# Reordering the ramp of batch 0 in a retention-plus-mixer kernel

## The chip, the cores and the metric

The kernel runs on one core of a Trainium2 chip. The metric is the time on the device, in microseconds, from the start to the end of the program; smaller is better. The numbers come from two sources: three timed runs, and one execution that the hardware profiler recorded. The engines are called PE (TensorE: matmuls and transposes), DVE (VectorE), ACT (ScalarE), POOL (GpSimd) and SP (SyncE, which here only issues transfers).

## What is computed

The inputs are q, k and v of shape 4 x 8 x 768 x 64 (batch, head, time, feature) in fp32, and four weights. A retention layer runs over time, and its output goes through a low-rank token mixer and a two-layer MLP with a residual:

```python
gamma = 1.0 - 2.0 ** (-5.0 - np.arange(H))
for t in range(S):
    state = gamma[None, :, None, None] * state + np.einsum('bhd,bhe->bhde', k[:, :, t], v[:, :, t])
    y[:, :, t] = scale * np.einsum('bhd,bhde->bhe', q[:, :, t], state)
...
h = xt @ U @ V                       # xt: x with time and features exchanged; rank 32 over 768 steps
u = x + h.transpose(0, 2, 1)
return u + np.maximum(u @ w_ch1, 0.0) @ w_ch2      # 512 -> 2048 -> 512
```

## The kernel before

**Chunks.** Each batch's 768 time steps are six chunks of 128. The recurrence is done chunk by chunk with matmuls. For chunk c, `ret_k` (L262) scales k by a decay (`kd`), `ret_q` or `ret_q0` scales q (`qd`), `ret_v` (L274) casts v on ACT (`vb`). kd and qd are transposed by PE (`kT`, `qT`), `ret_S` (L347) multiplies them into scores, `ret_mask` (L361) masks the scores on DVE in two halves of 0.68 us (`a`), `ret_sum` (L392) adds k times v of this chunk to one running PSUM bank, `ret_state` (L403) turns that bank into the masked bf16 `state` on DVE, and `ret_O` (L367) makes the chunk's output from qT with the state of the chunk before and from `a` with vb; ACT evicts it (`x`, L385). Since all six chunks add to one bank, `ret_sum` of chunk c+1 waits until `ret_state` of chunk c has read it.

**The ramp.** Before the first MLP matmul, batch 0 needs all its chunks, the low-rank product (`mix_P`, which needs `Ub`, and `mix_x`, `mix_h`, which need `Vb`) and the first columns of w1. This stretch is written out by hand at L564 to L641: the order of the calls is the order of the instructions on each engine, and each engine works strictly in that order. In batch 0 the loads of q come in pairs of chunks, 512 KB each, with even and odd rows apart (`load_q0`, L173); `ret_q0(i, eng)` (L302) scales the even half on one engine and the odd half on the other, `ret_Tq0(i, eng)` (L310) transposes both into one bank and evicts them into `q0T` with one strided copy of 1024 columns, by DVE for pair 0 and by ACT for pairs 1 and 2. `ret_Tk0(c)` (L324) transposes kd and evicts kT with ACT. `run_idle(n)` (L194) issues n matmuls on zeros into a bank that nobody reads. `cast_v` (L248) casts the mixer's V to bf16 on DVE; `spread_v` (L251) spreads it with PE and ACT.

**Queues.** All loads of batch 0 are issued by SP in the order of the list at L178: k0, q pair 0, k1, k2, V, q pair 1, k3, v0, q pair 2, k4, v1, k5, v2 to v5, then U. w1 and w2 are loaded and cast by POOL's own queue (`load_w1`, `load_w2`). At L601 POOL first copies one column of a v tile into `Ub`, so that the w1 loads behind it are not issued until that tile has landed; then come two w1 loads, `setup_u` (which waits for U), and the rest. POOL carries out in order: kd of each chunk, one half of each q pair, that gate, the weight loads, and later kd and qd of the other batches.

**The other batches.** The MLP of batch b runs as 32 slots of four matmuls (`mlp1`) and 48 slots of mostly two (`mlp2`); the retention of batch b+1 is put between them by slot number (`S_at`, `O_at`, `mix_at`, L644 to L680). The loads of batch 1 wait for a one-column ACT instruction at slot 14 of batch 0 (L138). From batch 2 on the transposes are done by DMA, issued by SP (L296); the scores of chunks 2 and 3 are put at slot 36.

Of the kernel before, what the change touches and what calls it, by code (L numbers as in the profile page):

```python
# [10 lines left out]
bf16 = mybir.dt.bfloat16  # L11
AF = mybir.ActivationFunctionType
# [35 lines left out]
def kernel(  # L48
# [20 lines left out]
    NP = H // 2  # L69
# [84 lines left out]
    Ub = wts.tile([P, NCK, RK], bf16)  # L154
# [16 lines left out]
    t0 = {}  # L171
# [3 lines left out]
        nc.sync.dma_start(out=q0f[:, i].rearrange("p h e d -> p h (e d)"),  # L175
                          in_=q[0, :, ds(2 * P * i, 2 * P)].rearrange("h (p e) d -> p h (e d)", e=2))

    for what in ("k0", "q0", "k1", "k2", "V", "q1", "k3", "v0", "q2", "k4", "v1", "k5", "v2", "v3",  # L178
                 "v4", "v5"):
        if what == "V":  # L180
            nc.sync.dma_start(out=Vf, in_=moe_V)
        elif what[0] == "q":
            load_q0(int(what[1]))
        else:
            load_one(t0, 0, int(what[1]), k if what[0] == "k" else v, what[0] + "_n")
# [8 lines left out]
    def run_idle(n):  # L194
        w = bank(0)
        for _ in range(n):
            matmul(w, idle[:, :P], idle, DM, start=True, stop=True)
# [50 lines left out]
    def cast_v():  # L248
        nc.vector.tensor_copy(out=Vs, in_=Vf)
# [24 lines left out]
    def ret_v(b, c):  # L274
        vb = rmid.tile([P, H, D], bf16, tag="vb", name=f"vb_{b}_{c}", bufs=6)
        nc.scalar.activation(vb, rc[b, c]["v_n"], AF.Copy)  # L276
        bal.book("A", 0.63)
        rc[b, c]["vb"] = vb
# [23 lines left out]
    def ret_q0(i, eng):  # L302
        t0["qd", i] = []
        for e in (0, 1):
            d = rmid.tile([P, H, D], bf16, tag="qd", name=f"qd0_{i}_{e}", bufs=4)
            eng[e].tensor_tensor(d, t0["q", i][:, :, e],  # L306
                                 Gq0[:, 2 * i + e].unsqueeze(2).to_broadcast([P, H, D]), op=ALU.mult)
            t0["qd", i].append(d)

    def ret_Tq0(i, eng):  # L310

        tp = bank(1, bf16, 2 * DM)
        for e, d in enumerate(t0["qd", i]):
            for n in range(NP):
                nc.tensor.transpose(tp[:, ds(e * DM + n * P, P)], d[:, ds(2 * n, 2)], ident)
                bal.mm(P)
        o = q0T[:, :, ds(2 * P * i, 2 * P)].rearrange("p n (t e) -> p e n t", e=2)
        src = tp.rearrange("p (e n t) -> p e n t", e=2, n=NP)
        if eng == "A":
            nc.scalar.activation(o, src, AF.Copy)  # L320
        else:
            nc.vector.tensor_copy(out=o, in_=src)

    def ret_Tk0(c):  # L324
        r = rc[0, c]
        o = rmid.tile([P, NP, P], bf16, tag="qkT", name=f"kT_0_{c}", bufs=6)
        tp = bank((2, TP)[c % 2], bf16, 2 * DM)[:, :DM]
        for p in range(NP):
            nc.tensor.transpose(tp[:, ts(p, P)], r["kd"][:, ds(2 * p, 2)], ident)
            bal.mm(P)  # L330
        r["kT"], r["qT"] = o, q0T[:, :, ts(c, P)]
        nc.scalar.activation(o.rearrange("p n t -> p (n t)"), tp, AF.Copy)  # L332

    def ret_T(b, c):
        if by_dma(b):
# [11 lines left out]
    def ret_S(b, cs, masks=True, bks=(SA, SB)):  # L347

        for c, bks in zip(cs, (bks, (OB, TP if by_dma(b) else 2))):
            r = rc[b, c]  # L350
            r["s"] = [bank(i) for i in bks]
            for p in range(NP):
                for e in (0, 1):
                    matmul(r["s"][e][:, ts(p, P)], r["kT"][ds(D * e, D), p],
                           r["qT"][ds(D * e, D), p], 80, start=True, stop=True)
        for c in cs:
            rc[b, c]["a"] = rmid.tile([P, 2, NP, P], bf16, tag="a", name=f"a_{b}_{c}", bufs=5)
            for e in (0, 1) if masks else ():
                ret_mask(b, c, e)

    def ret_mask(b, c, e):  # L361
        r = rc[b, c]
        nc.vector.tensor_tensor(r["a"][:, e], r["s"][e].rearrange("p (n t) -> p n t", n=NP), mask4,  # L363
                                op=ALU.mult)
        bal.book("V", 0.69)
# [197 lines left out]

    ret_k(0, 0, G)  # L564
    ret_Tk0(0)
    run_idle(3)
    ret_q0(0, (V, G))
    ret_Tq0(0, "V")
    ret_k(0, 1, G)
    ret_Tk0(1)  # L570
    run_idle(3)
    ret_S(0, [0])
    ret_k(0, 2, G)
    ret_Tk0(2)
    ret_S(0, [1], bks=(OB, ST))
    run_idle(4)
    ret_q0(1, (G, V))
    ret_Tq0(1, "A")
    ret_k(0, 3, G)
    ret_Tk0(3)  # L580
    cast_v()
    run_idle(2)
    ret_S(0, [2])
    ret_v(0, 0)
    spread_v()
    ret_sum(0, 0)
    ret_state(0, 0)
    ret_q0(2, (G, V))
    ret_S(0, [3])
    run_idle(2)  # L590
    ret_Tq0(2, "A")
    ret_k(0, 4, G)
    ret_v(0, 1)
    ret_Tk0(4)
    ret_O(0, 0, False)
    run_idle(2)
    ret_sum(0, 1)
    ret_state(0, 1)
    ret_k(0, 5, G)

    nc.gpsimd.tensor_copy(out=Ub[:, 0, :1], in_=t0["v_n", 2][:, 0, :1])  # L601
    load_w1(0, 256)
    load_w1(256, 256)
    setup_u()
    load_w1(512, 512)
    ret_S(0, [4])
    ret_Tk0(5)
    run_idle(1)
    ret_v(0, 2)
    ret_O(0, 1, False)  # L610
    ret_sum(0, 2)
    ret_state(0, 2)


    c = NCK - 3
    ret_v(0, c)
    ret_S(0, [NCK - 1], masks=False)
    ret_mask(0, NCK - 1, 0)
    ret_v(0, c + 1)
    ret_sum(0, c)  # L620
    ret_state(0, c)
    ret_O(0, c - 1, False)
    ret_mask(0, NCK - 1, 1)
    ret_O(0, c, False, (TP,))
    ret_v(0, c + 2)
    ret_sum(0, c + 1)
    ret_state(0, c + 1)
    ret_O(0, c + 1, False)
    for cc, bk in ((0, 1), (1, 2), (2, SA), (3, TP)):
        mix_x(0, 0, cc, bk)  # L630
    ret_O(0, c + 2, False, (SB, 0))
    mix_P(0, list(range(NCK - 1)), (OB, ST))
    mix_P(0, [NCK - 1])
    for cc, bk in ((0, SB), (1, 0)):
# [9 lines left out]
    for b in range(B):  # L644
        nxt = b + 1 < B
        slots = mlp1_slots(b)
        n1 = len(slots)
        side = {}
        set_banks([0, 1, 2, SA, SB, OB])
        if b == 0:  # L650
            taken.update({i: n for n, i in enumerate((1, 2, SA, TP, SB, 0, OB))})
            set_banks([1, 2, SA, TP, SB, 0, OB])
            order = [0, 2, 1, 3] + list(range(4, len(slots)))
            slots = [slots[i] for i in order]
            for i, s in ((1, 2), (2, 3)):
                put(side, i, lambda s=s: load_w1(512 * s, 512))
            for s in range(4):
                put(side, 4 + s, lambda s=s: load_w2(s))
            for c in range(NCK):
                put(side, 14, lambda c=c: load_chunk(1, c))  # L660
            at, lead, mix_at = [n1 + 7 + 5 * c for c in range(NCK)], 4, n1 + 38
            S_at = {(0, 1): n1 + 14, (2, 3): n1 + 24, (4,): n1 + 30, (5,): n1 + 35}
            O_at = [n1 + i for i in (19, 22, 29, 32, 35, 38)]
        if b:

            slots = slots[:12:2] + slots[1:12:2] + slots[12:]
        if b and nxt:
            set_banks([0, 1, 2])
            at, lead, mix_at = [10 + 4 * c for c in range(NCK)], 5, n1 + 24
            S_at = {(0, 1): 27, (2, 3): 36, (4, 5): 46}  # L670
            O_at = [32, 35, 42, 45, 52, 55]
        if nxt:
            ret_side(b + 1, at, lead, S_at, O_at, side)
            put(side, n1, lambda: set_banks([0, 1], [2]))
            put(side, mix_at, lambda: use.update(mix=[2, SA, SB]))
            mix_side(b + 1, mix_at, side)
        if b == 1:
            for c, i in ((3, 0), (4, 7), (5, 15)):
                put(side, i, lambda c=c: load_chunk(2, c))
        weave(slots + mlp2_slots(b), side)  # L680
# [30 lines left out]
```

## Time and profile before

| what | us |
|---|---|
| three timed runs, median (lowest to highest) | 231.39 (230.69 to 231.39) |
| profiled execution: its own time | 231.24 |
| profiled execution: span from first to last instruction | 229.5 |
| first matmul of the MLP of batch 0 starts at | 31.18 |
| PE busy in the span | 219.4 (96%) |
| ACT, DVE, POOL busy in the span | 113.8, 82.3, 55.2 |

The 1.7 us between the time and the span lie around the program. All other times are counted from the span's start. In the answers, a timeline line is: start, duration, engine, line, operation, tiles, count, and in brackets how long the engine had been idle and what ended that. A line of the chain of waits is: start, duration, what. "Landing" is the time at which a transfer's data are all there, "issue" that at which its queue began to issue it.

### The profile page before, as it was taken

Reading aid. Unit: us, or ns where it says so; the run is one execution under the profiler, and the core shown is the slowest. Engines: PE = TensorE matmul, PEld = TensorE weight load, DVE = VectorE, ACT = ScalarE, POOL = GpSimd, SP = SyncE. Lnnn points to the kernel's source line nnn. Section 1 sums busy time; section 2 is a strip of 40 time slices with the busy share of each in tenths; the row PEclk is TensorE's granted clock in tenths of the full one; section 3 lists DMA queues with packets and bytes.
Section 4 is the critical chain, followed back from the end, with each engine's and each line's share of the span. In section 5 each row is a group of like instructions: output and inputs, shape, how many; then the busy total and the mean of one; then the engine's idle time right before and its main releaser. Section 6 shows DMA issues by size and latency. Waiting matters only on the chain.

```text
span 229.5 us, 4198 instructions
## 1 busy us (share of the span) xinstructions
PE 219.4 (96%) x1698; PEld 123.8 (54%) x1698; DVE 82.3 (36%) x153; ACT 113.8 (50%) x220; POOL 55.2 (24%) x63
## 2 busy tenths in 40 slices
PE   7777899999999999999999999999999999999995
PEld 3234766655556456556555456556554456654454
DVE  5367740002677450006673720016674510001222
ACT  3256877772137457776233617767234447770000
POOL 2665540026545330413034601050000000000000
PEclk9889999999999999999999999999999999999999
DMA  7999899999999987968599969845411640001122
GB/s 174 236 239 208 108 205 202 194 220 225 219 198 254 203 228 180 196 143 151 91 225 227 263 149 212 186 96 111 96 46 48 137 138 3 0 0 46 56 85 91
DMA packets 102324, 34.95 MB, mean 152 GB/s; under 512 B 91264, under 2 KB 99328, under 8 KB 102304
## 3 DMA queue, kind: packets, MB, share of 16 engines
q1 hardware_dynamic: 97552, 30.49, 62.5%
q0 software_dynamic: 4752, 4.19, 11.7%
q8 instruction: 13, 0.21, 0.4%
q14 instruction: 7, 0.06, 0.1%
HBM read 27.46 MB, written 6.29 MB: 147 GB/s over the span
## 4 chain that ended last, share of the span: by engine, by line
PE 83%; DMA 6%; DVE 3%; ACT 2%; SPq 2%; POOL 2%; issue 1%; POOLq 0%
PE bk L115 81%; DMA q0f<-in_q_dram 2%; DMA qkT<-kd 2%; DMA q_n<-in_q_dram 2%; SPq L296 1%; DVE a L363 1%; PE bk L341 1%; ACT q0T L320 1%; DVE state L407 1%; POOL qd L306 1%; DVE qd L306 1%; ACT kT L332 0%; POOL qd L270 0%; SPq L140 0%; POOL kd L265 0%
## 5 line engine op out<-in xcount | busy, mean ns | idle before, releaser
L115 PE MATMUL bk<-w2b,gT 128*128 128x512 bf16 (+2 forms) x416 | 92.0, 363 | 0.0
L115 PE MATMUL bk<-uT,w1b 128*128 128x384 bf16 x512 | 84.4, 326 | 0.1
L120 ACT ACTIVATE gT<-bk 128x384 bf16<-128x384 f32 x126 | 61.9, 491 | 31.7 <-PE bk L115 31.6
L115 PEld LDWEIGHTS <-w1b 128*128 128x128 bf16 x512 | 49.9, 98 | 33.5 <-issue 0.5
L115 PEld LDWEIGHTS <-gT 128*128 128x128 bf16 x416 | 37.9, 98 | 37.7 <-issue 0.8
L363 DVE TENSOR_TENSOR a<-bk,mask 128x512 bf16<-128x512 f32 x48 | 30.1, 684 | 39.9 <-PE bk L115 39.6
L265 POOL TENSOR_TENSOR kd<-k_n,Gk 128x512 bf16<-128x512 f32 x24 | 25.0, 1043 | 78.5 <-DMA k_n<-in_k_dram 67.5
L507 DVE TENSOR_TENSOR res<-bk,res 128x512 f32<-128x512 f32 (+2 forms) x17 | 10.7, 627 | 46.6 <-PE bk L115 46.6
L385 ACT ACTIVATE x<-bk 128x512 bf16<-128x512 f32 x23 | 13.6, 596 | 23.7 <-PE bk L115 23.7
L270 POOL TENSOR_TENSOR qd<-q_n,Gq 128x512 bf16<-128x512 f32 x18 | 18.8, 1043 | 10.5 <-DMA qkT<-qd 9.3
L407 DVE TENSOR_TENSOR state<-bk,bmask 128x512 bf16<-128x512 f32 x20 | 13.8, 690 | 13.2 <-PE bk L115 13.1
L276 ACT ACTIVATE vb<-v_n 128x512 bf16<-128x512 f32 x24 | 14.4, 623 | 0.0
L476 ACT ACTIVATE x<-res 128x512 bf16<-128x512 f32 x15 | 9.3, 631 | 6.8 <-DVE res L474 6.5
L115 PEld LDWEIGHTS <-qkT 64*128 64x128 bf16 (+1 forms) x204 | 8.4, 95 | 7.7 <-issue 3.2
L474 DVE TENSOR_TENSOR res<-bk,x 128x512 f32<-128x512 f32 x15 | 9.8, 688 | 6.3 <-PE bk L115 6.2
L124 DVE COPY qkT<-bk 128x1024 bf16<-128x1024 bf16 x3 | 2.1, 692 | 26.4 <-PE bk L341 26.4
L115 PE MATMUL bk<-idle 128*128 128x512 bf16 x26 | 10.0, 518 | 1.2 <-DVE idle L192 1.2
L115 PE MATMUL bk<-vb,kd 128*128 128x128 bf16 x80 | 7.8, 219 | 2.2 <-ACT vb L276 1.5
L115 PE MATMUL bk<-vb,a 128*128 128x64 bf16 x192 | 9.5, 193 | 0.0
L120 ACT ACTIVATE qkT<-bk 128x1024 bf16<-128x1024 bf16 x3 | 3.1, 1024 | 12.7 <-PE bk L341 12.7
L115 PE MATMUL bk<-P_sb,Vb 128*128 128x512 bf16 x24 | 9.1, 380 | 0.0
L115 PEld LDWEIGHTS <-a 128*128 128x128 bf16 x192 | 8.0, 98 | 0.5
(71 smaller groups left out, 105.5 us busy)
## 6 DMA issues: line engine op xcount, KB each, us to landing
k_n<-in_k_dram SPq DMA_DIRECT2D x24, 256.0 KB, 5.2
v_n<-in_v_dram SPq DMA_DIRECT2D x24, 256.0 KB, 5.2
out_dram<-res SPq DMA_DIRECT2D x23, 256.0 KB, 2.6
q_n<-in_q_dram SPq DMA_DIRECT2D x18, 256.0 KB, 5.0
w2b<-in_moe_w_ch_dram POOLq DMA_DIRECT2D x4, 512.0 KB, 14.7
q0f<-in_q_dram SPq DMA_DIRECT2D x3, 512.0 KB, 5.2
w1b<-in_moe_w_ch_dram POOLq DMA_DIRECT2D x3, 512.0 KB, 8.0
w1b<-in_moe_w_ch_dram POOLq DMA_DIRECT2D x2, 256.0 KB, 5.2
```

The source lines that it names most:

```text
L115: nc.tensor.matmul(o, l, r, **kw)
L120: nc.scalar.activation(o, i, AF.Relu if relu else AF.Copy)
L265: eng.tensor_tensor(kd, k_n, Gk[:, c].unsqueeze(2).to_broadcast([P, H, D]), op=ALU.mult)
L270: eng.tensor_tensor(qd, rc[b, c]["q_n"], Gq[:, c].unsqueeze(2).to_broadcast([P, H, D]), op=ALU.mult)
L276: nc.scalar.activation(vb, rc[b, c]["v_n"], AF.Copy)
L306: eng[e].tensor_tensor(d, t0["q", i][:, :, e], Gq0[:, 2 * i + e].unsqueeze(2).to_broadcast([P, H, D]), op=ALU.mult)
L363: nc.vector.tensor_tensor(r["a"][:, e], r["s"][e].rearrange("p (n t) -> p n t", n=NP), mask4, op=ALU.mult)
L385: nc.scalar.activation(xs[b][:, c], o[0], AF.Copy)
L407: nc.vector.tensor_tensor(sb, ps.rearrange("p (n t) -> p n t", n=NP), bmask4, op=ALU.mult)
L474: nc.vector.tensor_tensor(u, h, xs[b][:, j], op=ALU.add)
L476: nc.scalar.activation(xs[b][:, j], u, AF.Copy)
L507: nc.vector.tensor_tensor(o, chp.pop((b, j)), o if by_token(b, j) else xs[b][:, j, ds(lo, w)], op=ALU.add)
```

## The change

Seven edits, all in the ramp of batch 0 but the last:

- q pair 1 is loaded right after k1, ahead of k2 and V.
- The two halves of pair 0 go to two PSUM banks, each evicted on its own: the even half by DVE, the odd half by ACT. Pair 0's transposes have three idle matmuls between the halves, pair 2's have two.
- `ret_q0(1)` and `ret_Tq0(1)` move ahead of kd of chunk 2; the scores of chunk 2 move ahead of kT of chunk 3, and `cast_v` ahead of those scores.
- kT of chunks 4 and 5 is evicted by DVE rather than ACT; pair 2 is scaled and transposed after the masks of chunk 3.
- The gate of w1 waits for v of chunk 4 rather than of chunk 2.
- The tail (chunks 1 to 5) is written out in a new order: each `ret_O` from chunk 1 to 4 now stands ahead of the next chunk's scores or beside the next sum, as the diff shows. There are 41 idle matmuls instead of 26.
- In batches 1 and 2 the slots of the next batch's retention move by one: scores of chunks 2 and 3 from slot 36 to 37, of 4 and 5 from 46 to 47, the outputs of chunks 2 to 5 and the mixer by one too.

```diff
-    for what in ("k0", "q0", "k1", "k2", "V", "q1", "k3", "v0", "q2", "k4", "v1", "k5", "v2", "v3",
+    for what in ("k0", "q0", "k1", "q1", "k2", "V", "k3", "v0", "q2", "k4", "v1", "k5", "v2", "v3",
...
+    def copy_by(eng, o, i):
+        if eng == "A":
+            nc.scalar.activation(o, i, AF.Copy)
+        else:
+            nc.vector.tensor_copy(out=o, in_=i)
+
+    def ret_Tq0(i, bks, between=0):
+
+        tp = [bank(bk, bf16, 2 * DM) for bk in bks]
+        o = q0T[:, :, ds(2 * P * i, 2 * P)].rearrange("p n (t e) -> p e n t", e=2)
         for e, d in enumerate(t0["qd", i]):
+            t = tp[e % len(tp)]
+            if e and between:
+                run_idle(between)
             for n in range(NP):
-                nc.tensor.transpose(tp[:, ds(e * DM + n * P, P)], d[:, ds(2 * n, 2)], ident)
+                nc.tensor.transpose(t[:, ds((e if len(tp) == 1 else 0) * DM + n * P, P)],
+                                    d[:, ds(2 * n, 2)], ident)
                 bal.mm(P)
...
+        if len(tp) == 2:
+            for e, eng in ((0, "V"), (1, "A")):
+                copy_by(eng, o[:, e], tp[e][:, :DM].rearrange("p (n t) -> p n t", n=NP))
         else:
+            copy_by("A", o, tp[0].rearrange("p (e n t) -> p e n t", e=2, n=NP))
...
+    def ret_Tk0(c, eng="A"):
...
+        copy_by(eng, o.rearrange("p n t -> p (n t)"), tp)
...
     ret_Tk0(0)
+    run_idle(6)
+    ret_q0(0, (V, G))
+    ret_Tq0(0, (1, OB), 3)
     run_idle(3)
-    ret_q0(0, (V, G))
-    ret_Tq0(0, "V")
     ret_k(0, 1, G)
+    ret_q0(1, (G, V))
     ret_Tk0(1)
-    run_idle(3)
     ret_S(0, [0])
+    run_idle(4)
+    ret_Tq0(1, (1,))
     ret_k(0, 2, G)
     ret_Tk0(2)
     ret_S(0, [1], bks=(OB, ST))
+    cast_v()
     run_idle(4)
-    ret_q0(1, (G, V))
-    ret_Tq0(1, "A")
+    ret_S(0, [2])
     ret_k(0, 3, G)
     ret_Tk0(3)
-    cast_v()
     run_idle(2)
-    ret_S(0, [2])
     ret_v(0, 0)
     spread_v()
     ret_sum(0, 0)
     ret_state(0, 0)
+    ret_S(0, [3])
+    ret_O(0, 0, False)
+    run_idle(4)
     ret_q0(2, (G, V))
...
-    ret_Tq0(2, "A")
     ret_k(0, 4, G)
     ret_v(0, 1)
-    ret_Tk0(4)
-    ret_O(0, 0, False)
-    run_idle(2)
+    ret_Tq0(2, (1,), 2)
     ret_sum(0, 1)
     ret_state(0, 1)
+    ret_Tk0(4, "V")
+    run_idle(2)
+    ret_O(0, 1, False)
     ret_k(0, 5, G)
-    nc.gpsimd.tensor_copy(out=Ub[:, 0, :1], in_=t0["v_n", 2][:, 0, :1])
+    nc.gpsimd.tensor_copy(out=Ub[:, 0, :1], in_=t0["v_n", 4][:, 0, :1])
...
     ret_S(0, [4])
-    ret_Tk0(5)
-    run_idle(1)
+    ret_Tk0(5, "V")
     ret_v(0, 2)
-    ret_O(0, 1, False)
+    run_idle(2)
     ret_sum(0, 2)
     ret_state(0, 2)
...
+    ret_S(0, [5], masks=False)
+    ret_mask(0, 5, 0)
+    ret_v(0, 3)
+    ret_O(0, 2, False)
+    ret_sum(0, 3)
+    ret_mask(0, 5, 1)
+    ret_state(0, 3)
+    ret_v(0, 4)
+    ret_O(0, 3, False, (TP,))
+    ret_sum(0, 4)
+    ret_state(0, 4)
+    ret_v(0, 5)
+    ret_O(0, 4, False)
...
-            at, lead, mix_at = [10 + 4 * c for c in range(NCK)], 5, n1 + 24
-            S_at = {(0, 1): 27, (2, 3): 36, (4, 5): 46}
-            O_at = [32, 35, 42, 45, 52, 55]
+            at, lead, mix_at = [10 + 4 * c for c in range(NCK)], 5, n1 + 25
+            S_at = {(0, 1): 27, (2, 3): 37, (4, 5): 47}
+            O_at = [32, 35, 43, 46, 53, 56]
```

More of the change, by code (lines that the diff above doesn't have):

```diff
@@ L308, in ret_q0 @@
             t0["qd", i].append(d)
-    def ret_Tq0(i, eng):
-        tp = bank(1, bf16, 2 * DM)
+    def copy_by(eng, o, i):
[6 more added lines that the diff above has]
+        o = q0T[:, :, ds(2 * P * i, 2 * P)].rearrange("p n (t e) -> p e n t", e=2)
         for e, d in enumerate(t0["qd", i]):
+            t = tp[e % len(tp)]
+            if e and between:
+                run_idle(between)
             for n in range(NP):
-                nc.tensor.transpose(tp[:, ds(e * DM + n * P, P)], d[:, ds(2 * n, 2)], ident)
+                nc.tensor.transpose(t[:, ds((e if len(tp) == 1 else 0) * DM + n * P, P)],
+                                    d[:, ds(2 * n, 2)], ident)
                 bal.mm(P)
[L317 to L320, printed above, removed]
-        else:
-            nc.vector.tensor_copy(out=o, in_=src)
-    def ret_Tk0(c):
+        if len(tp) == 2:
+            for e, eng in ((0, "V"), (1, "A")):
+                copy_by(eng, o[:, e], tp[e][:, :DM].rearrange("p (n t) -> p n t", n=NP))
+        else:
+            copy_by("A", o, tp[0].rearrange("p (e n t) -> p e n t", e=2, n=NP))
+    def ret_Tk0(c, eng="A"):
         r = rc[0, c]
@@ L331, in ret_Tk0 @@
         r["kT"], r["qT"] = o, q0T[:, :, ts(c, P)]
-        nc.scalar.activation(o.rearrange("p n t -> p (n t)"), tp, AF.Copy)
+        copy_by(eng, o.rearrange("p n t -> p (n t)"), tp)
     def ret_T(b, c):
@@ L587 @@
     ret_state(0, 0)
+    ret_S(0, [3])
+    ret_O(0, 0, False)
+    run_idle(4)
     ret_q0(2, (G, V))
-    ret_S(0, [3])
-    run_idle(2)
-    ret_Tq0(2, "A")
     ret_k(0, 4, G)
     ret_v(0, 1)
-    ret_Tk0(4)
-    ret_O(0, 0, False)
-    run_idle(2)
+    ret_Tq0(2, (1,), 2)
     ret_sum(0, 1)
     ret_state(0, 1)
+    ret_Tk0(4, "V")
+    run_idle(2)
+    ret_O(0, 1, False)
     ret_k(0, 5, G)
-    nc.gpsimd.tensor_copy(out=Ub[:, 0, :1], in_=t0["v_n", 2][:, 0, :1])
+    nc.gpsimd.tensor_copy(out=Ub[:, 0, :1], in_=t0["v_n", 4][:, 0, :1])
     load_w1(0, 256)
@@ L606 @@
     ret_S(0, [4])
-    ret_Tk0(5)
-    run_idle(1)
+    ret_Tk0(5, "V")
     ret_v(0, 2)
-    ret_O(0, 1, False)
+    run_idle(2)
     ret_sum(0, 2)
     ret_state(0, 2)
[L615 to L628, printed above, removed]
+    ret_S(0, [5], masks=False)
[11 more added lines that the diff above has]
+    ret_O(0, 4, False)
     for cc, bk in ((0, 1), (1, 2), (2, SA), (3, TP)):
         mix_x(0, 0, cc, bk)
-    ret_O(0, c + 2, False, (SB, 0))
+    ret_O(0, 5, False, (SB, 0))
     mix_P(0, list(range(NCK - 1)), (OB, ST))
```

## The prediction

> **What bounds the kernel now.** I read the page's head first: PE is the busy engine, and its row sags only at the left.
>
> ```profile
> span 229.5 us, 4198 instructions
> ...
> PE   7777899999999999999999999999999999999995
> ```
>
> Each digit is a 40th of the span, 5.7 us: the first five are short. So I asked for the chain of waits (start, duration, what), to see what holds the ramp and whether anything is lost later.
>
> ```profile
> 11.29 2.47 DVE a L363 x4
> 13.77 0.61 DVE qd L306
> ...
> 14.86 1.32 ACT q0T L320
> ...
> 19.61 1.32 ACT q0T L320
> 20.93 0.47 ACT vb L276
> 21.41 0.50 ACT kT L332
> ...
> 22.71 0.60 ACT kT L332
> 23.31 0.53 ACT vb L276
> ...
> 26.45 28.93 PE bk L115 x215
> ...
> 106.46 4.47 DMA qkT<-kd
> 110.93 0.05 issue
> 110.98 115.71 PE bk L115 x814
> ```
>
> From 26.45 (the last state sum, of chunk 4) PE is the chain, so whatever brings 26.45 forward brings the end forward, if nothing downstream breaks. Before it the chain goes through DVE and ACT: pair 1 of q is scaled only behind four mask halves (13.77), the 1.3 us eviction of q0T comes twice, and ACT puts vb and kT one behind the other. Later there is one loss, 0.45 us at 111. The timeline shows both engines of the first q pair, that loss, and the load of q pair 1:
>
> ```profile
> 6.56 0.69 DVE L306 TENSOR_TENSOR qd<-q0f,Gq 128x512 bf16<-128x512 f32 x1 [2.61 <-DMA q0f<-in_q_dram]
> 6.60 1.55 POOL L306 TENSOR_TENSOR qd<-q0f,Gq 128x512 bf16<-128x512 f32 x1 [1.47 <-DMA q0f<-in_q_dram]
> ...
> 110.98 0.40 PE L115 MATMUL bk<-qkT 64*128 64x128 bf16 x8 [0.45 <-DMA qkT<-kd]
> ```
>
> ```profile
> 6.16 0.43 SPq L175 DMA_DIRECT2D q0f<-in_q_dram  x1
> ```
>
> Last, the busy times in 2 us windows, whose columns after the stretch are PE, PEld, DVE, ACT, POOL busy, granted clock, DMA share, GB/s:
>
> ```profile
> 10.00:12.00 2.00, 2.00 (x20) 0.97 (x20) 0.72 (x2) 0.41 (x2) 0.94 (x2) 0.50 1.32 220
> ```
>
> PE ran at half clock there, after 6 to 10 us in which it was mostly idle.
>
> **The change, part by part: a new chain to the sum at 26.45.**
>
> *q pair 1 ahead of k2 and V.* Landings now (issue plus the tile's time to landing): k1 1.87 + 5.8 = 7.7, k2 2.91 + 6.2 = 9.1, V 4.22 + 5.4 = 9.6, q pair 1 6.16 + 5.1 = 11.2. The three behind k1 take 3.5 us for 256 + 96 + 512 KB. By bytes pair 1 takes 2.1 us, by its own step behind V 1.6, by pair 2's step behind v0 (13.5 to 15.3) 1.8. So it lands at 9.3 to 9.8; I take 9.6. On SP's queue the two transfers it passes move back: k2 to about 10.9, V to 11.4. k2 is first wanted at 11.25 (below), V's cast at 14.2: covered.
>
> *POOL.* kd1 still ends at 9.15. The half of pair 1 starts at 9.7 (0.13 behind the landing, as 6.60 behind 6.47) and now runs beside DVE's half, as pair 0 did: 1.55 us, not the 1.04 of the page's L270 and L265 rows. It ends at 11.25, kd2 (1.04) at 12.3. Bounds: 1.04 to 1.55 for the half; I take 1.55, the same pair of operations.
>
> The Trainium skill, page "SBUF — State Buffer", section "Who interferes with whom", speaks against this placement: a VectorE operation with two SBUF inputs and a GpSimd operation that reads SBUF exclude each other, whoever issues first. By the rule POOL would have waited from 6.60 to 7.25 and taken 1.69; the row says 1.55. By the rule the sum would be 0.14 worse, or, if POOL goes first, DVE would be held 1.04, ahead of masks that have 1.6 us to spare.
>
> *PE, then DVE.* kT2's transposes go at 12.35, S(1) behind them at 12.57 (0.23 for four transposes, as 9.21 to 9.44); S takes 0.40, so mask a(1) starts at 13.0. DVE operations in a row start 0.60 apart (11.28 to 13.68 for four). Two masks and the cast of V (0.54, 0.46 to the next start) bring a(2) to 14.66 and its end to 15.9.
>
> *ACT beside it.* Pair 1's eight transposes end at 11.95, q0T (1.31) at 13.3, kT2 (0.50 more) at 13.8, S(2) at 14.25: ready before DVE at 14.66. kT3 is transposed behind S(2), 14.1 to 14.45, evicted by 15.1; vb0 to 15.6, sum(0) to 16.05. So state(0) starts at 16.05, 0.2 behind the masks: here ACT is the later one. Now it starts at 17.84.
>
> *The second half.* From 16.05: state 0.60, two masks of a(3) 1.20, half of pair 2 0.68: 18.55. Its transposes 0.45, q0T by ACT 0.04 + 1.31: 20.35. S(4) 0.05 + 0.40: a(4) starts at 20.85 (now 22.48). Then DVE: two masks 1.20, kT5 0.35, state(2) 0.60, two masks 1.20, state(3) 0.68: 24.9; sum(4) at 24.95.
>
> *kT by DVE* is not in the trace. Nearest rows: DVE L124, 1024 columns in 0.692 (half: 0.35), ACT L332, 512 columns in 0.60. I take 0.43, nearer the row of the same engine, 0.35 to the next start; kT4 hides behind q0T, kT5 does not, so the bounds are 0.1 better and 0.2 worse. ACT is freed of both, so vb1 and vb2 no longer stand in a row with kT.
>
> *The split eviction of pair 0.* Halves of a 1.31 us copy: 0.65 to 1.31 each. q0T is whole at 9.4 to 9.95; S(0) follows kT1's transposes at 9.45, a(0) stands behind DVE's half of pair 1 (to 10.4) and ends by 11.7, against 13.0 for a(1). Off the path, worth nothing by itself.
>
> *15 more idle matmuls.* At 0.215 each 3.2 us of PE, at full clock all in gaps: six end at 7.2 (first transposes 7.3), three and three fit before 8.2 and 9.2, four end at 10.6 (11.3), four at 13.6 (13.85). At half clock they no longer fit; that is a rival. They also fill 6 to 10 us, which was idle ahead of the half clock.
>
> *w1 held back.* The gate moves from v2 (20.1) to v4, 17.28 + 5.8 = 23.0 or earlier, since the first w1 loads no longer share the transfer engines. Behind it on POOL: two w1 issues (0.9, 0.75), the cast of U, the other weights, later kd of batch 1. U lands by 25.6 as now, and POOL is free at 24.9, so the later weights are issued no later than now (26.1). The first w1 piece, issued at 23.2, lands 4.8 to 5.6 later, 28.0 to 28.8; the MLP would want it at 31.18 - 1.5 = 29.7, the second piece four slots (2.6) later. Hidden, by 0.9 us.
>
> *Slot 36 to 37.* The wait at 111 is for kT of chunk 3, whose chain (SP's transposes from 94) hangs on PE's earlier work and moves with it. A slot is two 512-column matmuls, 0.43 us of useful work put ahead: 0.43 of the 0.45 goes. Bounds 0 to 0.45. The other slots move with nothing waiting; the nearest, the DMA transposes of batch 2's uT, land 138.5 for a use at 135.84 + 6 x 0.65 = 139.7.
>
> *Downstream cover.* Batch 1's chunk 5 is scaled by 70.2 on POOL and transposed at 72.6: 2.4 of slack, 0.9 after the shift. SP is free for uT at 81.0 and waits for ACT until 82.86: 1.9 of slack, 0.4 after.
>
> Sum: 26.45 - 24.95 = 1.5, plus 0.43, is 1.93. From the profiled time, 231.24 - 1.93 = **229.3**. The median of the runs, 231.39, is 0.15 above that execution, so this is also the forecast for the median within what runs scatter. I call "no change" anything within 0.3%, 0.7 us: about what a measurement of this kernel can tell.
>
> **Rivals.**
>
> *Half clock in the new ramp (230.3).* For: the row at 0.50. Against: the new idle matmuls fill the idle stretch ahead of it. If 9.7 to 13.1 runs at half clock, four idle matmuls and twelve transposes ahead of S(1) take 3.0 instead of 1.5 us; pair 1's q0T starts 0.8 to 0.9 later, kT2, S(2), kT3, vb0, state(0) with it. 229.3 + 0.9 = 230.2, and 0.1 for S itself. The Trainium skill, page "TensorE: Matmul & The Clock Gate", Part 1, says that the window over which activity is judged is free-running, 3.4 us long: so the stretch may fall elsewhere from one execution to the next. The trace shows one such stretch, and no second execution.
>
> *The transfer is not early (230.8).* If pair 1 still lands at 11.2, the chain starts 1.6 later and the ramp gains nothing: 231.24 - 0.43. Against: the queue lands in order in every row.
>
> *Given back downstream (229.9 to 230.7).* The loads of 41 to 80 run at 200 GB/s and may not move with PE. Then the shift is cut to the 0.9 of chunk 5, or the wait at 111 returns: 231.24 - 0.9 - 0.43 = 229.9, without the 0.43 and at a slack of 0.5, 230.7.
>
> *Slower: w1 is late (232.6).* v5, U and both w1 pieces now share one stretch. The third and fifth w1 loads took 5.3 and 9.8 us behind others. If the first piece takes 9.8, it lands at 33.0, the MLP starts 33.0 - 31.18 = 1.8 later than now, less 0.43: 231.24 + 1.4. It decides from 8.4 us on, where this loss equals the 0.43; up to 6.5 it costs nothing. Against: 0.86 MB is then in flight, where the load of 9.8 was the last of 1.5 MB of weights issued in a row.
>
> **How the numbers follow.** Likeliest, 0.68: 229.3, its own range 228.7 (pair 1 at 9.3, POOL at 1.04) to 230.0 (9.8, kT 0.60, wait not removed). Half clock 0.11, not early 0.03, given back 0.07, slower 0.11. The range that leaves out two in ten: 228.6 to 230.8. Faster (under 230.7): 0.68 + 0.11 + 0.05 = 0.84; slower (over 232.1) 0.10, nearly all of the w1 rival; the rest, 0.06, within.
>
> **What would show it.** Right: the MLP's first matmul near 29.7; POOL's second qd half at 9.7, 1.5 long; a(4) at 20.9; sum(4) at 25.0; no wait above 0.1 near 109; clock 1.00 from 10 to 13. Wrong: a granted clock of 0.50 there; a wait for w1b or Ub ahead of the MLP; new waits for qkT in batch 1 or 2.

## The result, and the profile after

| | kernel before | changed kernel |
|---|---|---|
| timed runs, median (lowest to highest) | 231.39 (230.69 to 231.43) | 229.16 (228.92 to 229.47) |
| profiled execution: its time, its span | 231.24, 229.5 | 229.47, 227.7 |
| q pair 0 and q pair 1 landed | 6.47, 11.22 | 5.65, 8.66 |
| last state sum (chunk 4) | 26.45 | 24.26 |
| first matmul of the MLP of batch 0 | 31.18 | 28.98 |
| first piece of w1 landed | 25.12 | 26.80 |
| MLP of batch 0 to MLP of batch 1 | 54.00 | 54.00 |
| batch 1 to batch 2 | 50.66 | 50.67 |
| batch 2 to batch 3 | 49.07 | 49.42 |

The changed kernel takes 0.9912 of the time before, with a 95% interval of 0.9888 to 0.9935: 2.2 us faster at the medians, 1.77 in the two profiled executions (231.24 - 229.47). The head of the page of the changed kernel:

```profile
span 227.7 us, 4234 instructions
...
PE   7898899999999999999999999999999999999995
```

Three digits of the first five have risen, so the gain lies in the ramp; the row says nothing finer. The chain of waits of the changed kernel does (start, duration, what):

```profile
8.72 1.55 POOL qd L306
10.27 1.01 POOL kd L265
...
13.72 0.60 ACT kT L312
14.32 0.53 ACT vb L276
...
18.29 1.33 ACT q0T L312
...
24.26 28.93 PE bk L115 x215
...
130.48 0.51 SPq L520
131.08 2.44 DMA uT<-x
133.65 1.47 PE bk L115 x8
...
154.18 4.85 DMA qkT<-kd
159.07 65.78 PE bk L115 x438
```

The ramp now hangs on q pair 1's half on POOL; kT and vb in a row on ACT and one q0T of 1.33 remain. PE is the chain from 24.26 instead of 26.45. The old stop at 110.98 is gone, and two have come: at 133.65, where the MLP of batch 2 waits for a DMA transpose (uT, the MLP's input with time and features exchanged; six transposes per batch, the first three for the first half of the time steps) that was issued behind an output store (L520), and one at 159.07, where the scores of chunks 2 and 3 wait for a transposed kd. The timeline of the changed kernel has the steps on DVE and POOL (start, duration, engine, line, operation, tiles, count):

```profile
8.68 0.69 DVE L306 TENSOR_TENSOR qd<-q0f,Gq 128x512 bf16<-128x512 f32 x1 [0.97 <-DMA q0f<-in_q_dram]
8.72 1.55 POOL L306 TENSOR_TENSOR qd<-q0f,Gq 128x512 bf16<-128x512 f32 x1 [0.39 <-DMA q0f<-in_q_dram]
...
10.23 1.04 POOL L265 TENSOR_TENSOR kd<-k_n,Gk 128x512 bf16<-128x512 f32 x1
...
19.12 0.41 DVE L314 COPY kT<-bk 128x512 bf16<-128x512 bf16 x1
```

and its 2 us windows (columns after the stretch: PE, PEld, DVE, ACT, POOL busy, granted clock, DMA share, GB/s) show full clock where it was 0.50 before:

```profile
10.00:12.00 2.00, 1.38 (x22) 0.92 (x21) 0.57 (x1) 1.01 (x1) 1.65 (x3) 1.00 1.36 218
```

**How to split the gain.** Pair 0 of q itself landed 0.82 earlier in this execution (6.47 - 5.65), so part of the ramp's 2.20 (31.18 - 28.98) is not the new chain's. I therefore count the ramp from that landing: 24.71 before, 23.33 after. So 1.38 is the chain, 0.82 the landing. Batch 1 wins the 0.45 of the old wait and loses 0.46 at uT (0.01 longer in all), batch 2 is 0.35 longer: 0.82 + 1.38 - 0.01 - 0.35 = 1.84, as PE's last matmul moved (226.46 to 224.62). This is an account of one pair of executions; and the one of the kernel before held a stretch at half clock, so part of the 1.38 may be the clock.

### The profile page after: what moved, and what is told of

Its sections match the earlier page's. It is cut to its first block, busy times and chain, and to the rows that moved or that the text cites. A ratio compares the mean times of both kernels' runs of the same rounds, so it can differ in the third digit from the quotient of the medians.

```text
span 227.7 us, 4234 instructions
## 1 busy us (share of the span) xinstructions
PE 220.0 (97%) x1713; PEld 123.9 (54%) x1713; DVE 82.3 (36%) x155; ACT 114.0 (50%) x219; POOL 55.4 (24%) x63
## 4 chain that ended last, share of the span: by engine, by line
PE 77%; SPq 7%; DMA 7%; DVE 3%; ACT 1%; issue 1%; POOL 1%; POOLq 0%
PE bk L115 75%; SPq L140 3%; DMA q0f<-in_q_dram 3%; SPq L296 2%; DMA qkT<-kd 2%; DVE a L373 1%; PE bk L351 1%; DMA qkT<-qd 1%; DMA uT<-x 1%; SPq L520 1%; DVE res L517 1%; DVE state L417 1%; POOL qd L306 1%; ACT q0T L312 1%; POOL kd L265 1%
## 5 line engine op out<-in xcount | busy, mean ns | idle before, releaser
L115 PE MATMUL bk<-idle 128*128 128x512 bf16 x41 | 12.4, 430 | 1.2 <-DVE idle L192 1.2
```

The costliest lines, as they stand in the source:

```text
L115: nc.tensor.matmul(o, l, r, **kw)
```

## The experiments

All of them at a glance. "Ramp" is the MLP's first matmul less the landing of pair 0; "b1" and "b2" run from MLP to MLP as above; the last column is PE's wait for uT at the start of the MLP of batch 2, or within it. The last five columns come from one profiled execution each; the kernel before stood beside the runs at 231.73 (first four), 232.06 (next four), 231.83 (last four).

| run | median us | ratio, 95% interval | pair 0 | ramp | b1 | b2 | uT wait |
|---|---|---|---|---|---|---|---|
| kernel before | 231.39 | 1 | 6.47 | 24.71 | 50.66 | 49.07 | none |
| the change | 229.16 | 0.9912, 0.9888 to 0.9935 | 5.65 | 23.33 | 50.67 | 49.42 | 0.46 |
| e1_oldslots | 230.14 | 0.9918, 0.9890 to 0.9945 | 6.35 | 23.50 | 50.75 | 49.71 | 0.18 + 0.48 |
| e2_slots23 | 232.48 | 1.0060, 1.0039 to 1.0081 | 5.76 | 23.23 | 51.84 | 50.88 | none |
| e3_before_newslots | 231.37 | 0.9993, 0.9966 to 1.0020 | 6.13 | 24.70 | 50.62 | 49.10 | 0.41 |
| e4_q1late | 231.84 | 1.0003, 0.9971 to 1.0034 | 6.72 | 24.91 | 50.73 | 49.10 | 0.53 |
| e5_mixslot | 229.70 | 0.9889, 0.9837 to 0.9942 | 6.11 | 23.24 | 50.04 | 49.14 | none |
| e6_fewidle | 229.88 | 0.9903, 0.9868 to 0.9939 | 5.78 | 23.30 | 50.61 | 49.20 | 0.40 |
| e7_onebank | 229.22 | 0.9866, 0.9820 to 0.9911 | 5.88 | 23.29 | 50.74 | 49.07 | 0.53 |
| e8_ramp2 | 230.61 | 0.9929, 0.9893 to 0.9965 | 5.88 | 24.09 | 51.05 | 49.11 | 0.85 |
| e9_kT_act | 230.12 | 0.9937, 0.9916 to 0.9958 | 6.38 | 24.06 | 50.14 | 49.11 | none |
| e10_before_q1early | 232.06 | 1.0012, 0.9991 to 1.0034 | 6.21 | 26.30 | 50.77 | 49.07 | none |
| e11_mix_vb0 | 229.64 | 0.9913, 0.9891 to 0.9934 | 6.43 | 22.93 | 50.08 | 49.70 | 0.47 |
| e12_change_again | 229.05 | 0.9892, 0.9872 to 0.9911 | 5.86 | 23.20 | 50.04 | 49.07 | none |

In the expectations, A is my own account at that time, and the other letters are its rivals; J, from the last runs, is that the new load order also brings pair 0's landing forward.

### Slots: e1, e2, e3

e1 is the change with all slots of before.

```diff
-            at, lead, mix_at = [10 + 4 * c for c in range(NCK)], 5, n1 + 25
-            S_at = {(0, 1): 27, (2, 3): 37, (4, 5): 47}
-            O_at = [32, 35, 43, 46, 53, 56]
+            at, lead, mix_at = [10 + 4 * c for c in range(NCK)], 5, n1 + 24
+            S_at = {(0, 1): 27, (2, 3): 36, (4, 5): 46}
+            O_at = [32, 35, 42, 45, 52, 55]
```

> The new ramp with the slot numbers of before (scores of chunks 2 and 3 at 36, 4 and 5 at 46, mixer one slot earlier). Theory A (the ramp alone gives the gain, the slots net nothing, since SP's stream of loads and transposes does not move with PE): 228.9 to 229.5; a PE wait of 0.4 to 0.9 us for qkT near 108.5 comes back, the wait of 0.46 us for uT at 133.65 goes. Rival B (the slots are worth their 0.43, as predicted): 229.6 to 229.9, the wait near 108.5 back and the one at 133.65 no smaller.

0.9918: nearly all the gain is there without the slots. The median, 230.14, lies above both ranges, in a set in which the kernel before was slower too (231.73). By the ratios the slots are worth 0.1 to 0.6 us (0.9912 and 0.9892 of the change against 0.9918, times 231.7), and the intervals overlap. The old loss near 110 shrank to 0.19 by itself, and the uT wait that A had going stayed: 0.18 at the start of the MLP, and 0.48 within it.

e2 moves only the scores of chunks 2 and 3.

```diff
-            S_at = {(0, 1): 27, (2, 3): 37, (4, 5): 47}
-            O_at = [32, 35, 43, 46, 53, 56]
+            S_at = {(0, 1): 27, (2, 3): 37, (4, 5): 46}
+            O_at = [32, 35, 43, 46, 52, 55]
```

The mixer is back at `n1 + 24` too.

> The new ramp, of the slots only chunks 2 and 3 moved (scores 37, outputs 43 and 46; scores of 4 and 5 at 46, mixer at the slot of before). Theory A: neither wait, since the third transpose of uT is again issued ahead of the output of token block 3: 228.5 to 228.8, gaps of PE after the ramp under 0.3 us in sum. Rival C (uT is late because all of SP's stream is late, whatever its order): the wait at 133.65 stays at 0.3 or more and the time at 229.0 to 229.2.

Slower by 0.6%. The timeline of e2 shows why:

```profile
114.26 2.48 DVE L373 TENSOR_TENSOR a<-bk,mask 128x512 bf16<-128x512 f32 x4 [0.93 <-PE bk L115]
...
116.20 0.38 PE L115 MATMUL bk<-state,qkT 128*128 128x128 bf16 x4 [1.75 <-DVE a L373]
```

With the scores of chunks 4 and 5 and the output of chunk 3 all at slot 46, the output wants the bank that those scores have just filled, and PE stands 1.75 us behind the masks, here and once more in batch 2 (167.29). The conflict is the experiment's own: it says why the later slots had to move along, and nothing of my theory.

e3 is the kernel before with the new slots (e1's diff the other way round).

> The ramp of before with the new slot numbers. Theory A: the wait at 110.98 goes (0.45), and at the later start of the MLP uT has 1.8 - 0.4 - 0.6 us of slack left, so no wait at 135.8: 230.8 to 231.1, at most 0.45 under before. Rival B': nothing, 231.2 to 231.5, another wait takes the place of the one removed.

No gain, 0.9993. The wait at 110.98 is gone, but in the timeline of e3 the same time is lost at uT:

```profile
135.45 4.75 PE L115 MATMUL bk<-uT,w1b 128*128 128x384 bf16 x28 [0.41 <-DMA uT<-x]
```

### What makes uT late: e5 and e12

SP's queue in the timeline of the kernel before, around the MLP of batch 2 (the duration is that of the issuing):

```profile
128.82 3.89 SPq L478 DMA_TRANSPOSE uT<-x  x3
132.80 0.53 SPq L510 DMA_DIRECT2D out_dram<-res  x1
133.42 3.84 SPq L478 DMA_TRANSPOSE uT<-x  x3
```

and in that of the changed kernel, with PE's wait and the scores of chunks 2 and 3 in the MLP of batch 2:

```profile
127.33 3.04 SPq L488 DMA_TRANSPOSE uT<-x  x2
130.46 0.53 SPq L520 DMA_DIRECT2D out_dram<-res  x1
131.08 5.16 SPq L488 DMA_TRANSPOSE uT<-x  x4
...
133.65 17.75 PE L115 MATMUL bk<-uT,w1b 128*128 128x384 bf16 x108 [0.46 <-DMA uT<-x]
...
158.54 0.93 PE L115 MATMUL bk<-qkT 64*128 64x128 bf16 x16
```

The mixer one slot later lets an output store into the queue ahead of the third transpose instead of behind it. That store takes 0.62 until the next issue (130.46 to 131.08); without it the third transpose would have landed at 132.9 instead of 133.52, ahead of the 133.19 at which PE was ready. That made the swap look like the cause. e5 puts only the mixer back.

```diff
-            at, lead, mix_at = [10 + 4 * c for c in range(NCK)], 5, n1 + 25
+            at, lead, mix_at = [10 + 4 * c for c in range(NCK)], 5, n1 + 24
```

> The change with the mixer back at the slot of before (n1 + 24), scores and outputs left at the new slots, so that the third uT transpose of batch 2 is again issued ahead of the output of token block 3. Theory A (that output, 0.6 us of SP's issue time, is what makes uT late): the wait of 0.46 us at the start of batch 2's MLP falls under 0.1, the wait at 111 stays away; MLP of batch 1 takes 50.2 to 50.3 instead of 50.66; time 0.3 to 0.5 under the changed kernel's ratio of 0.991, so 0.989. Rival C (all of SP's stream is late): the wait stays above 0.3 and the ratio at 0.991.

In the timeline of e5 three transposes stand together again, and PE doesn't wait:

```profile
127.13 4.33 SPq L488 DMA_TRANSPOSE uT<-x  x3
131.55 0.53 SPq L520 DMA_DIRECT2D out_dram<-res  x1
...
133.40 6.89 PE L115 MATMUL bk<-uT,w1b 128*128 128x384 bf16 x41
```

b1 fell to 50.04. I took the swap for the whole cause. e12, the changed kernel once more, contradicts that:

> The change itself once more beside the others: ratio 0.990 to 0.992, the last state sum 18.5 to 18.7 after the first q landing, MLP start 23.2 to 23.4 after it, a wait of 0.4 to 0.5 for uT at batch 2. By theory J pair 0 lands at 5.6 to 6.2.

```profile
126.31 2.96 SPq L488 DMA_TRANSPOSE uT<-x  x2
129.37 0.53 SPq L520 DMA_DIRECT2D out_dram<-res  x1
...
133.34 6.83 PE L115 MATMUL bk<-uT,w1b 128*128 128x384 bf16 x41
...
158.19 0.62 PE L115 MATMUL bk<-qkT 64*128 64x128 bf16 x16
```

In this timeline of the same kernel the order is swapped, and there is no wait. What differs is SP's lead, the time from the issue of its first uT until PE is ready for that MLP: 7.03 here (133.34 - 126.31), 5.86 in the first execution (133.19 - 127.33). The lead tells all 14 profiles apart. PE stopped for uT in the eight with a lead of 5.91 or less (the change, e1, e3, e4, e6, e7, e8, e11), and not in the six with 6.27 or more (the kernel before, e2, e5, e9, e10, e12).

The swap only chooses which transposes come late. With the store ahead of the third, PE stops at the start of the MLP. With the mixer at its old slot the store stands ahead of the fourth, and PE stops 24 matmuls later, where it first uses the second three: 0.48 in e1 at a lead of 5.72, 0.47 in e11 at 5.91. So it was its lead of 6.27 that kept e5 free. The reckoning with 132.9 above overlooks the sixth transpose, which landed at 137.46 in the first execution; without the stop PE would have used it at 137.25, 24 matmuls (4.06, the row of e11 below) after 133.19. Why the lead differs by over a microsecond between two executions of one kernel is open.

The stop at the scores is absent from e12 too: the 16 matmuls took 0.62 here and 0.93 in the first execution: these 0.31 are most of the 0.35 that batch 2 lost there. Where both stay away the slots do pay: b1 and b2 together are 99.11 against 99.73 before. These 0.62 are more than the 0.45 of idle time at 110.98, because the stop cost more than PE's idle time: in the timeline of the kernel before the sixteen scores there (the row at 110.14 here and that at 110.98 in the prediction) ran from 110.14 to 111.38, 1.24, and sixteen without a wait took 0.62:

```profile
103.15 0.62 PE L115 MATMUL bk<-qkT 64*128 64x128 bf16 x16
...
110.14 0.40 PE L115 MATMUL bk<-qkT 64*128 64x128 bf16 x8
```

But e12 gave 0.24 back in batch 0, which took 54.24 instead of 54.00, with a wait for POOL's qd of batch 1 at 70.57; from the first MLP to the last 0.38 is left. In time, e5 (229.70) is no better than the change (229.05, 229.16).

### The ramp: e4 and e10

e4 is the change with the load order of before, e10 the kernel before with the new load order alone (the same line the other way round).

```diff
-    for what in ("k0", "q0", "k1", "q1", "k2", "V", "k3", "v0", "q2", "k4", "v1", "k5", "v2", "v3",
+    for what in ("k0", "q0", "k1", "k2", "V", "q1", "k3", "v0", "q2", "k4", "v1", "k5", "v2", "v3",
```

> The change with the load order of before (q pair 1 behind k2 and V). Theory A (the early landing of pair 1 heads the new chain): pair 1 lands 1.5 to 2.0 later, near 10.5 to 11.2, sum(4) near 25.9 instead of 24.3, time 230.5 to 231.0. Rival D (the new order of the engines' work gives the gain and DVE and ACT would have caught up): sum(4) by 24.8, time at most 229.6.

> Before with the new load order alone. Theory A (order of loads and order of work only pay together): pair 1 lands 3.0 after pair 0, but DVE still scales it behind four masks, and k2 is later; MLP starts 24.6 to 25.1 after the first q landing, as before (24.7). Rival I (the load order alone carries the gain): 24.0 or less. Beside it, of the landing of pair 0 itself: theory J (the load issued fourth decides how early pair 0 lands): 5.6 to 6.2, as in most runs with q pair 1 fourth; rival (chance from one execution to the next): 6.1 to 6.7.

1.0003 and 1.0012: neither part is worth anything without the other. In e4 pair 1 lands 4.39 behind pair 0, and the new order of calls only waits for it (ramp 24.91, the last state sum at 26.90, later than A's 25.9). In e10 it lands 2.95 behind, but nothing uses that. POOL in the timeline of e10:

```profile
7.86 1.03 POOL L265 TENSOR_TENSOR kd<-k_n,Gk 128x512 bf16<-128x512 f32 x1
10.58 1.04 POOL L265 TENSOR_TENSOR kd<-k_n,Gk 128x512 bf16<-128x512 f32 x1 [1.68 <-DMA k_n<-in_k_dram]
11.58 1.04 POOL L306 TENSOR_TENSOR qd<-q0f,Gq 128x512 bf16<-128x512 f32 x1
```

kd of chunk 2 still stands ahead of pair 1's half, and k2 now lands at 10.51: pair 1 is there at 9.16 and is scaled at 11.58. The ramp of that execution, 26.30, is 1.6 longer than before, and its windows show half clock twice over:

```profile
12.00:14.00 2.00, 1.78 (x13) 0.86 (x13) 1.24 (x3) 0.60 (x1) 1.62 (x2) 0.50 1.09 273
...
20.00:22.00 2.00, 2.00 (x22) 1.60 (x21) 1.45 (x3) 1.05 (x1) 1.92 (x3) 0.50 1.37 220
```

Of e10's ten executions the four with a mean granted clock of 0.999 or more took 230.75 to 231.61, the six with 0.977 to 0.993 took 231.62 to 232.70: means of 231.26 and 232.48. So this profile overstates what the load order alone costs, and half clock in this ramp goes with 1.2 us. In e4 it is the same: four of ten executions at a mean clock of 0.993, six at 1.000, with mean times of 232.50 and 231.30. In the 55 executions of the change and the eight kernels that hold both parts it was never below 0.998. Of the 54 of the kernel before that stood beside the runs 36 were at 0.993 or less; set by set (27, 10 and 17 executions) their means were 0.40 above, 0.02 below and 0.28 above those of the rest. On J the runs give 6.47, 6.13 and 6.72 for pair 0's landing with k2 fourth, and 5.65 to 6.43, mean 6.03, in the eleven with pair 1 fourth. The means differ by 0.4, the ranges overlap: not settled.

### Single edits of the ramp: e6, e7, e9

e6 takes nine idle matmuls away.

```diff
-    run_idle(6)
-    ret_q0(0, (V, G))
-    ret_Tq0(0, (1, OB), 3)
     run_idle(3)
+    ret_q0(0, (V, G))
+    ret_Tq0(0, (1, OB))
```

> The change with nine idle matmuls fewer between 5 and 9 us: three instead of six behind kT0, none between the halves of pair 0, none behind them. Theory A (they keep the clock at full speed): a stretch of 3.4 us at half clock appears between 6 and 16 us, and the last state sum comes 19.1 to 19.6 after the first q landing instead of 18.6; 0.5 to 1.0 us slower than the change. Rival E (the clock does not depend on them): clock 1.00 throughout and 18.5 to 18.7.

A miss for the idle matmuls: ramp 23.30, and in the windows of e6 the clock stays full although PE is busy 0.98 and 1.48 of 2.00 from 6 to 10, where the changed kernel's is busy throughout and that of the kernel before was busy 1.12 and 1.19. All five executions of e6 were at a mean clock of 1.000.

```profile
6.00:8.00 2.00, 0.98 (x9) 0.45 (x8) 1.29 (x2) 0.22 (x2) 2.00 (x2) 1.00 1.18 271
8.00:10.00 2.00, 1.48 (x16) 0.76 (x16) 1.19 (x2) 1.29 (x2) 1.60 (x2) 1.00 1.29 231
```

e7 puts pair 0 back into one bank, with one DVE copy.

```diff
-    ret_Tq0(0, (1, OB), 3)
+    ret_Tq0(0, (1,), 3, "V")
```

> The change with pair 0 evicted as before, both halves from one bank in one DVE copy of 1.31 us. Theory A (the split is off the path): the masks of chunk 0 start later by up to 0.6, the last state sum still comes 18.5 to 18.8 after the first q landing; ratio 0.990 to 0.993. Rival F (the split carries part of the gain): 19.0 or more, ratio 0.994 or above.

0.9866 and a ramp of 23.29: the split eviction is worth nothing. Its timeline holds a by-product, the two halves of pair 1 in the other order:

```profile
8.95 1.04 POOL L306 TENSOR_TENSOR qd<-q0f,Gq 128x512 bf16<-128x512 f32 x1 [0.38 <-DMA q0f<-in_q_dram]
...
9.29 1.24 DVE L306 TENSOR_TENSOR qd<-q0f,Gq 128x512 bf16<-128x512 f32 x1
...
10.24 1.19 POOL L265 TENSOR_TENSOR kd<-k_n,Gk 128x512 bf16<-128x512 f32 x1 [0.26 <-DMA k_n<-in_k_dram]
```

The longer DVE copy delays DVE's half, POOL goes first and takes 1.04, and now DVE is the slow one.

e9 gives kT of chunks 4 and 5 back to ACT.

```diff
-    ret_Tk0(4, "V")
+    ret_Tk0(4)
...
-    ret_Tk0(5, "V")
+    ret_Tk0(5)
```

> The change with kT of chunks 4 and 5 evicted by ACT again. Theory A (ACT would be the later engine there): scores of chunk 4 wait for kT4 behind q0T, vb2 stands behind kT5; the last state sum comes 19.1 to 19.6 after the first q landing instead of 18.55; ratio 0.994 to 0.996. Rival H (DVE pays for them what ACT saves): 18.5 to 18.8, ratio 0.990 to 0.992.

230.12 against 229.05 for the change measured beside it: 1.07 us, and the intervals are apart (0.9916 to 0.9958, 0.9872 to 0.9911). The ramp is 24.06, 0.86 longer than e12's. ACT in the timeline of e9:

```profile
19.00 1.33 ACT L312 ACTIVATE q0T<-bk 128x1024 bf16<-128x1024 bf16 x1 [0.97 <-PE bk L325]
20.18 0.59 ACT L312 ACTIVATE kT<-bk 128x512 bf16<-128x512 bf16 x1
...
21.58 0.60 ACT L312 ACTIVATE kT<-bk 128x512 bf16<-128x512 bf16 x1 [0.33 <-PE bk L339]
22.08 1.14 ACT L276 ACTIVATE vb<-v_n 128x512 bf16<-128x512 f32 x2
```

kT of chunk 4 queues behind the long q0T and holds the scores of chunk 4; kT of chunk 5 stands ahead of vb, for which the sum of chunk 2 waits. Of the parts tried one by one, this is the largest after the load order.

### Trying for more: e8 and e11

e8 is a ramp order of my own: scores of chunk 1 ahead of pair 1's transposes, vb of chunk 0 ahead of kT of chunk 3, pair 2 scaled ahead of the masks of chunk 3, the scores of chunk 4 ahead of the sum of chunk 1. (Not in the lines below: idle matmuls moved, and the state of chunk 3 ahead of the second mask half of chunk 5.)

```diff
+    ret_S(0, [1], bks=(OB, ST))
+    run_idle(2)
     ret_Tq0(1, (1,))
     ret_k(0, 2, G)
     ret_Tk0(2)
-    ret_S(0, [1], bks=(OB, ST))
     cast_v()
...
-    ret_Tk0(3)
     ret_v(0, 0)
+    ret_Tk0(3)
     ret_sum(0, 0)
     ret_state(0, 0)
+    ret_q0(2, (G, V))
...
     ret_Tq0(2, (1,), 2)
+    ret_Tk0(4, "V")
+    ret_S(0, [4])
+    ret_v(0, 1)
     ret_sum(0, 1)
```

> A further order of the ramp: scores of chunk 1 ahead of pair 1's transposes, v0 cast ahead of kT3, sum and state of chunk 0 ahead of the scores of chunk 3, pair 2 scaled right behind state 0, scores of chunk 4 ahead of the sum of chunk 1. Theory A (the chain of DVE and ACT sets the ramp, landings of k5 and v2 to v5 come next): last state sum 17.7 to 18.2 after the first q landing instead of 18.6, and a part of it lost again to uT in batch 2: ratio 0.988 to 0.990. Rival G (the landings already set the second half of the ramp): 18.5 or more, ratio 0.991.

A miss: 230.61, ramp 24.09. The timeline of e8 shows two losses:

```profile
11.91 1.04 POOL L265 TENSOR_TENSOR kd<-k_n,Gk 128x512 bf16<-128x512 f32 x1 [0.35 <-DMA k_n<-in_k_dram]
...
12.10 1.26 DVE L249 CAST Vs<-Vf 32x768 bf16<-32x768 f32 x1
...
15.63 1.00 DVE L306 TENSOR_TENSOR qd<-q0f,Gq 128x512 bf16<-128x512 f32 x1
...
18.18 1.31 ACT L312 ACTIVATE q0T<-bk 128x1024 bf16<-128x1024 bf16 x1 [0.71 <-PE bk L325]
...
19.34 0.61 ACT L276 ACTIVATE vb<-v_n 128x512 bf16<-128x512 f32 x1
...
20.01 0.38 PE L115 MATMUL bk<-vb,kd 128*128 128x128 bf16 x4
```

On DVE the cast of V, 0.54 before, fell just behind the start of a kd on POOL and took 1.26; half of pair 2 took 1.00 instead of 0.68 behind POOL's half. Even so the masks of chunk 4 began a little earlier, 14.08 behind the landing of pair 0 (14.43 in the changed kernel). The larger loss is on ACT: vb of chunk 1 now stands behind the long q0T of pair 2, so the sum of chunk 1 came 14.13 behind that landing, against 12.44 where vb stands ahead of it (17.01 and 18.29 in the changed kernel). Every later sum waits in turn for the state before it, and the last was 0.8 late.

e11 is e5 with vb of chunk 0 ahead of kT of chunk 3 on ACT.

```diff
+    ret_v(0, 0)
     ret_Tk0(3)
...
-    ret_v(0, 0)
```

> The change with the mixer's slot of before, and with the cast of v0 ahead of kT3 on ACT. Theory A (kT3 and vb0 in a row on ACT hold state 0 by 0.3): state 0 starts right behind the masks of chunk 2, the last state sum 0.1 to 0.3 earlier, 18.2 to 18.4 after the first q landing (k5 lands late and holds the rest); no wait for uT; ratio 0.986 to 0.989. Rival G (the landings set it): 18.5 to 18.6.

The ramp fell to 22.93, 0.31 under e5's, the shortest of all, and the time did not: 229.64. In its timeline the gain is spent at uT:

```profile
133.44 4.06 PE L115 MATMUL bk<-uT,w1b 128*128 128x384 bf16 x24
137.97 4.22 PE L115 MATMUL bk<-uT,w1b 128*128 128x384 bf16 x25 [0.47 <-DMA uT<-x]
```

No version beat the change beyond the noise (the interval of e7's 0.9866 reaches to 0.9911).

## Why the prediction was right, and where it was not

The time, 229.3 forecast and 229.16 measured, came from the right main term and two errors that nearly cancelled: the slots gave less than their 0.43, and pair 0's landing gave 0.82 that no term held. That the number came so close was luck.

**The ramp's chain: right, 1.38 for 1.5.** Counted from pair 1's landing, the forecast had a(1) at +3.40, state(0) at +6.45, a(4) at +11.25 and sum(4) at +15.35; measured +3.43 (12.09 - 8.66), +6.65, +11.42 and +15.60. The missing 0.2 to 0.25 arose at state(0), where kT of chunk 3 and vb stand in a row on ACT (the lines at 13.72 and 14.32); e11 turned those two round and got 0.3 back. Pair 1 landed 3.01 behind pair 0, not 3.13. The rival "the transfer is not early" fell, and e4 shows what it would have been: no gain at all, so worse than the 230.8 it was priced at. That price took the slots' 0.43 as earned; e4 had a uT wait of 0.53 instead, and its ramp was 0.2 longer than before.

**q pair 1 passing k2: right, with little to spare.** k2 landed 1.28 behind pair 1, as the forecast had it (10.9 - 9.6), and POOL wanted it 0.33 later (10.27 - 9.94). So POOL's 1.55 rather than 1.04 for its half cost next to nothing: in e7, where it was 1.04, kd of chunk 2 then waited for k2 and, counted from pair 1's landing (8.88 there), ended at +2.55, against +2.61 here. The Trainium skill, page "SBUF — State Buffer", section "Who interferes with whom", calls the port pair that the two engines share an exclusive lock. A POOL operation held out until DVE's was done would have made 1.69; the rows say 1.55 here and before. The other statement of the page, that the order of issue decides who blocks, is what e7 shows: POOL first, and DVE's half takes 1.24 instead of 0.69, ending 0.54 behind POOL's (10.53 and 9.99).

**kT by DVE: right in size, 0.41 for 0.43.** The sum held it only as a cost on DVE; what it frees on ACT was folded into the chain, and e9 prices it at 0.86 of ramp and 1.07 of time.

**Split eviction of pair 0: right.** Halves of 0.73 and 0.74, off the path; e7.

**w1 held back: right, and the slower rival fell.** Issued at 22.36, the first piece landed at 26.80 (4.4 later), 2.2 ahead of the MLP rather than 0.9, since v of chunk 4 landed at 22.18 and not 23.0. The second landed at 28.85 for a use 2.6 behind the MLP's start. A gate left at chunk 2 was not tried.

**Idle matmuls against half clock: the reason given is not shown.** The forecast let them "fill 6 to 10 us, which was idle ahead of the half clock"; but PE was busy 1.12 and 1.19 of 2.00 there, so "mostly idle" was a misreading. The clock did stay full, but with nine of them gone too (e6). As to the rival's price, 0.9: in e4 and e10 a lower clock went with 1.2 us, in the three sets of the kernel before with 0.40, nothing and 0.28, and in e3 half clock at 18.1 to 21.5 left the ramp at 24.70. No profile of the kernel before at full clock exists, so how much of the 1.38 is the clock stays open. What keeps the clock full is only narrowed down: the early load and the order that uses it have to be there together.

**The slots: this step failed.** It said that 0.43 of the wait at 111 goes and that "the other slots move with nothing waiting; the nearest, the DMA transposes of batch 2's uT, land 138.5 for a use at 139.7". The wait did go, and it had cost 0.62 rather than 0.45. What failed is the cover for uT: the use at 139.7 was worked out from PE's old time, 135.84, without the ramp's gain. The shift was taken off the cover of batch 1's uT and not off that of batch 2's. In the first execution PE was ready 2.65 earlier (135.84 to 133.19) while SP's first uT came only 1.5 earlier (128.82 to 127.33). The third transpose, which the first matmuls need, had landed 1.82 ahead of PE before (134.02 for 135.84). It lost 0.62 to the store, 1.16 to SP's shorter lead and a net 0.37 in the other issues, the first of which took 1.73 instead of 1.22, and landed 0.33 late. With the mixer at its old slot the sixth would have been the late one, as in e1 and e11. Measured: no gain in batch 1 and 0.35 lost in batch 2, instead of 0.43 gained; in e12, without the stops, 0.62 gained in these two and 0.24 lost in batch 0. It is the rival "given back downstream" in a small dose, and its sign "new waits for qkT" showed as well, at 159.07, in the first execution only.

**What filled the gap** was not in the sum: pair 0's landing, 0.82 earlier than in the kernel before's execution, with its cause open (J).

## What to carry to other kernels

An earlier load and an order of calls that uses it are one edit: each alone was worth nothing here (1.0003 and 1.0012), together 0.989 to 0.991. After a gain at the front, follow every in-order queue that does not move with the critical engine, in each later stage and not in the first alone; how far the queue runs ahead of that engine counts for more than which issues change places in it. Count a ramp from the landing of its first load, since that differs by up to a microsecond between executions and hides what an edit of a few tenths does; and profile the same kernel twice before calling a wait of half a microsecond present or gone.

## What the runs showed of the hardware

- DVE and POOL both reading SBUF at the same time: in these rows the engine that starts second is the one that pays. POOL second: 1.55 instead of 1.04, and 1.19 in e7 (the row at 10.24). DVE second: 1.24 or 1.00 instead of 0.69 (e7, e8), and a cast of 32 x 768 took 1.26 instead of 0.54. Each of these five ends 0.12 to 0.15 earlier than if it had begun only when the first was done.
- Half clock came in stretches of 3.41 us, at 9.65 in the kernel before, 18.06 in e3, 11.82 and 18.65 in e10: the same ramp, another place each time. The Trainium skill, page "TensorE: Matmul & The Clock Gate", Part 1, has a free-running window of 3.4 us, and these rows agree. No profile with the change's own load order and order of calls, whole or with one edit undone, showed such a stretch in the ramp, e6 with its emptier PE included.
- One kernel's SP stream ran 5.86 or 7.03 us ahead of PE at the same point, in two executions whose clock was full in both.
